# Second level of Strassen's algorithm for two products of the first GEMM, with another order of the visits to its outputs

## The chip, the cores and the metric

The kernel runs on one core of a Trainium2 chip. The metric is the device time of one execution in microseconds (us), the median of several runs. Five engines work side by side, each on its own queue in order: PE (TensorE, matmuls; PEld is its weight loads), DVE (VectorE), ACT (ScalarE), POOL (GpSimd) and SP (SyncE, which here only issues DMAs). They wait for one another through semaphores.

## The reference, cut to what matters

```python
gamma = 1.0 - 2.0 ** (-5.0 - np.arange(H))            # B, H, S, D = 4, 8, 768, 64
for t in range(S):                                      # retention
    state = gamma * state + np.einsum('bhd,bhe->bhde', k[:, :, t], v[:, :, t])
    y[:, :, t] = scale * np.einsum('bhd,bhde->bhe', q[:, :, t], state)
x = y.transpose(0, 2, 1, 3).reshape(B * S, H * D)       # 3072 x 512
h = x @ w_in                                            # 512 x 2048: the first GEMM
g = np.where(h > 0, h, np.exp(np.minimum(h, 0)) - 1)    # ELU
out = g @ w_out                                         # 2048 x 512: the second GEMM
```

All of it is fp32.

## The kernel before, in words

The 3072 tokens are worked through in six blocks of 512 (`tb` 0 to 5; `TB`, `TH` is half of it). For each block the kernel computes the retention (`scores` L256, `states` L275, `outputs` L299), which leaves x transposed in `xb`, then the first GEMM, ELU, and the second GEMM. The order of the instructions on every engine is written out by hand (`manual_schedule`): generators yield at places where other work is put between, and the main loop (L792 to L855) interleaves them. The retention of block tb+1 is cut into five `retention_step`s and lies inside block tb.

Block 0 uses plain matmuls while the weights are decoded. From block 1 on, each GEMM is a Strassen product in Winograd's form. With quarters a of the weights and b of the data, there are seven products M1 = a11 b11, M2 = a12 b21, M3 = s4 b22, M4 = a22 t4, M5 = s1 t1, M6 = s2 t2, M7 = s3 t3, where s and t are sums of quarters. The outputs are C11 = M1+M2, C12 = M1+M6+M5+M3, C21 = M1+M6+M7+M4 and C22 = M1+M6+M7+M5.

- *First GEMM* (`first(n)`, L489; its matmuls are on L501). The 1024 rows of an output quarter are cut into four `n` of 256. For every n, `strassen` (L459) runs the products in the order 1, 2, 6, 7, 5, 3, 4. One product is four matmuls of 128x128 weights with 256 columns and fills one PSUM bank of 128x512. Products 1, 6, 5 and 3 add up in one bank (`pa`, two buffers); 7 and 4 in another (`pd`, one buffer); 2 has `pb`. ACT copies the partial sums out (`kept`, L449 to L451), DVE adds (`plus`, L454 to L456). `elu` (L374) does two activations on ACT (L377, L378) and one operation on DVE (L380), which is held back in the list `later` until the next call. After C12 two subtractions (L513) make T3 and T1, inputs of the second GEMM. `combine_x` (L359) makes t1 to t4 on DVE (L360); `combine_w_in` (L433) makes s1 to s4 once, in block 1.
- *Second GEMM*. In block 1 it is one level (`second`, L554, matmuls on L559); `combine_w_out` (L540) makes the sums for a second level and stores them to `scratch2` in DRAM. From block 2 on it is two levels (`second_twice`, L604, matmuls on L622): each of the seven products is again seven, each of four matmuls with 128 columns into 128x128 of a bank. `inputs` (L607 to L615, operations on L611) makes the inner sums on DVE, `copy` (L628, L630) is a small copy on ACT and `add` (L633, L634) an addition on DVE. The weights of each small product come from DRAM through a ring of 11 tiles `wq` of 256 KB; `fetch_small` (L591) issues the next fetch on SP's queue after each small product. The ring and the pool of the inputs take the memory of the early pools (`stage`, `t4`) once block 1 is over.

The ending of `first(3)` (products 3 and 4) is laid into the start of the second GEMM, and the ending of the last inner product of the second GEMM into the start of the next block.

In block 1 the main loop calls `combine_w_in(n+1)` beside `first(n)`, one operation at each step, and loads the inputs of block 2 (`bring`: `load` on SP's queue and `scale_v`, L238 on POOL). At the end of block 1 it calls `combine_x` and then fills the ring. From block 2 on it issues the loads for the next block at n=0 and n=1, retention steps 0 and 1 at n=2 and 3, and steps 2 to 4 inside the second GEMM behind its inner products 2, 6 and 7.

Of the kernel before, what the change touches and what calls it, by code (L numbers as in the profile page):

```python
# [2 lines left out]

# [5 lines left out]
FP32 = mybir.dt.float32  # L9
# [7 lines left out]
def kernel(  # L17
# [3 lines left out]
    w_bits: bass.AP,  # L21
    scratch: bass.AP,
    scratch2: bass.AP,
    out: bass.AP,
    dims,
):

# [74 lines left out]

    w_a = [const.tile([P, 2, 2, 2, P], FP32, name=f"w_a{n}") for n in range(NQ)]
    w_b = [const.tile([P, 2, 2, 2, P], FP32, name=f"w_b{n}") for n in range(NQ)]
    w_s = [const.tile([P, 3, 2, 2, P], FP32, name=f"w_s{n}") for n in range(NQ)]
    NPIECE = 2 * NQ + NF  # L110
    staged, prepared, decoded = [], [], []

# [108 lines left out]


    xb = const.tile([P, 4, TB], FP32, name="xb")
    xt = [const.tile([P, 2, TH], FP32, name=f"xt{n}") for n in range(4)]
    carry = [const.tile([P, HP, D], FP32, name=f"carry{n}") for n in range(2)]
    held = {}

# [128 lines left out]

    half = [slice(0, TH), slice(TH, TB)]

    def combine_x():  # L359
        sub = lambda o, x, y: nc.vector.tensor_tensor(out=o, in0=x, in1=y, op=ALU.subtract)  # L360
        b11, b12, b21, b22 = (xb[:, 2 * r : 2 * r + 2, half[t]] for r in range(2) for t in range(2))
        sub(xt[0], b12, b11)
        sub(xt[1], b22, xt[0])
        sub(xt[2], b22, b12)
        sub(xt[3], b21, xt[1])


    later = []
# [2 lines left out]
        while later:  # L371
            later.pop(0)()

    def elu(g, h):  # L374

        r = epool.tile([P, 512], FP32, name="r", tag="r")
        nc.scalar.activation(r, h, AF.Relu, scale=-1.0)  # L377
        nc.scalar.activation(r, r, AF.Exp, scale=-1.0)  # L378
        flush()
        later.append(lambda: nc.vector.scalar_tensor_tensor(g, r, -1.0, h, ALU.add, ALU.max))  # L380

    def plain_first():

# [167 lines left out]
                scratch2[j - 1, :, 1024 * k : 1024 * k + 1024], x.rearrange("p k f d -> p (k f d)")  # L551
            )

    def second(tb):  # L554
        def product(j, ps, begin):
            ws = fetched.pop((tb, j))
            for f in range(NF):
                for d in range(2):
                    nc.tensor.matmul(  # L559
                        ps[:, d, :], lhsT=ws[:, 2 * d + f // 4, f % 4, :], rhs=gq[INPUT2[j]][:, f, :],  # L560
                        start=(begin and f == 0 and d == 0), stop=(f == NF - 1), skip_group_check=True,
                    )
            at = ORDER2.index(j) + 3
            if j in (2, 6):
                next_input(j)
            combine_w_out(j, ws)
            if at < 7:
                fetch(tb, ORDER2[at])

        def use(name, h):  # L570
            r, t = int(name[1]) - 1, int(name[2]) - 1
            if name == "C12":
                ot = hpool.tile([P, 2, TH], FP32, name="h", tag="h")
                nc.scalar.copy(ot, h)
                h = ot
            nc.sync.dma_start(out[tb, r, t].rearrange("p d c -> p (d c)"), h.rearrange("p d c -> p (d c)"))

        return strassen(product, use, None)
# [1 line left out]


    RING = 11
    USE = [(1, k) for k in (1, 2, 6, 7, 5)]
    for at in range(1, 7):
        j, before = ORDER2[at], ORDER2[at - 1]
        USE += [(j, 1), (j, 2), (before, 3), (before, 4), (j, 6), (j, 7), (j, 5)]
    USE += [(4, 3), (4, 4)]
    to_fetch = [(tb, j, k) for tb in range(2, NTB) for j, k in USE]
    small_w = []

    def fetch_small():  # L591
        if not to_fetch:
            return
        tb, j, k = to_fetch.pop(0)
        t = ring.tile([P, 4, P], FP32, name="wq", tag="wq")
        if k in (1, 2, 4):
            q = 4 * SLOT[j] + {1: 0, 2: 1, 4: 3}[k]
            nc.sync.dma_start(t.rearrange("p f d -> p (f d)"), scratch[q])
        else:
            n = {5: 0, 6: 1, 7: 2, 3: 3}[k]  # L600
            nc.sync.dma_start(t.rearrange("p f d -> p (f d)"), scratch2[j - 1, :, 512 * n : 512 * n + 512])
        small_w.append(((tb, j, k), t))

    def second_twice(tb, behind_last):  # L604
        quarter = lambda x, r, t: x[:, 4 * r : 4 * r + 4, P * t : P * t + P]
        ts, kept2 = {}, {}

        def inputs(j):
            x, t = gq[INPUT2[j]], tpool.tile([P, 4, 4, P], FP32, name="ts", tag="ts")
            b11, b12, b21, b22 = (quarter(x, a, b) for a in range(2) for b in range(2))  # L610
            sub = lambda o, x, y: nc.vector.tensor_tensor(out=o, in0=x, in1=y, op=ALU.subtract)  # L611
            sub(t[:, 0], b12, b11)
            sub(t[:, 1], b22, t[:, 0])
            sub(t[:, 2], b22, b12)
            sub(t[:, 3], b21, t[:, 1])  # L615
            ts[j] = {1: b11, 2: b21, 3: b22, 4: t[:, 3], 5: t[:, 0], 6: t[:, 1], 7: t[:, 2]}

        def product(j, k, ps, begin):
            name, w = small_w.pop(0)
            assert name == (tb, j, k)  # L620
            for f in range(4):
                nc.tensor.matmul(  # L622
                    ps, lhsT=w[:, f, :], rhs=ts[j][k][:, f, :], start=(begin and f == 0), stop=(f == 3),
                    skip_group_check=True,
                )
            fetch_small()
# [9 lines left out]
        def inner(j):  # L636
# [16 lines left out]
            yield  # L653
            product(j, 3, pa, False)
            nc.scalar.copy(res[:, 0, 1], pa)
            product(j, 4, pd, False)
            add(res[:, 1, 0], pd, u2)
            sum_up(j, res.rearrange("p d t c -> p (d t c)"))
# [23 lines left out]
                add(m, kept2[7], m)  # L682
                store("C21", m)

        inputs(1)
        before = iter(())
        for at, j in enumerate(ORDER2):
            cur = inner(j)
            next(cur)
            if j == 1:  # L690
                yield "tail"
            for _ in before:
                pass
            if j == 2:
                next_input(2)
            if j == 5:
                next_input(6)
            if j == 1:

                next(cur)  # L700
                yield "elu"
                next(cur)
            if at + 1 < 7:
                inputs(ORDER2[at + 1])
            else:
                behind_last()
            if j != 1:
                next(cur)
                next(cur)
            before = cur  # L710
            yield j
        for _ in before:
            pass


    prepare(2)
# [51 lines left out]
            for _ in combine_w_in(0):  # L768
                pass
    combine_x()  # L770
    for j in ORDER2[:3]:
        fetch(1, j)


    def retention_step(tb, step):
# [8 lines left out]
        elif step < 5:  # L784
            outputs_step(tb, step - 2)

    def bring(m):
        load(m)
        scale_v(m)

    tail = iter(())
    for tb in range(1, NTB):  # L792
        more = tb + 1 < NTB
        at_once = more and tb > 1
        for n in range(NQ):
            if at_once and n == 0:
                bring((tb + 1) * CPB)
                bring((tb + 1) * CPB + 1)
            if at_once and n == 1:
                bring((tb + 1) * CPB + 3)  # L800
            cur = first(n)
            for at in range(3):
                next(cur)

            for _ in tail:
                pass
            if at_once and n >= 2:
                retention_step(tb + 1, n - 2)
            side = combine_w_in(n + 1) if tb == 1 and n + 1 < NQ else iter(())
            for s in cur:  # L810
                next(side, None)
                if s == "gap":
                    break
            for _ in side:
                pass
            tail = cur
            if at_once and n == 0:
                bring((tb + 1) * CPB + 2)
            if more and not at_once:
                bring((tb + 1) * CPB + n)  # L820
        if tb == 1:
            cur = second(tb)
            next(cur)
            next(cur)
            for _ in tail:
                pass
            flush()
            for step, s in enumerate(cur):
                retention_step(tb + 1, step)
            combine_x()  # L830
            tail = iter(())
            early.close()
            ring = ctx.enter_context(tc.tile_pool(name="ring", bufs=RING))
            tpool = ctx.enter_context(tc.tile_pool(name="tpool", bufs=2))
            for _ in range(RING):
                fetch_small()
        else:
            cur = second_twice(tb, combine_x if more else lambda: None)
            next(cur)
            for s in tail:  # L840
                if s == "last":
                    break
            next(cur)
            for _ in tail:
                pass
            flush()
            for step, j in enumerate(cur):

                if 0 < step < 4:
                    retention_step(tb + 1, step + 1)  # L850
                if j == ORDER2[-1]:
                    break
            tail = cur
    for _ in tail:
        pass  # L855

# [45 lines left out]
```

## Time and profile before

| | us |
|---|---|
| median of 5 runs | 661.21 (659.58 to 662.9) |
| the profiled execution: its own time | 662.32 |
| its span, from the first to the last instruction | 660.6 |
| PE busy | 639.8 |
| DVE busy | 434.2 |
| ACT busy | 228.9 |
| POOL busy | 23.8 |
| block 2, first to last product (253.23 to 356.08) | 102.85 |
| block 3 (356.08 to 458.27) | 102.19 |
| block 4 (458.27 to 560.46) | 102.19 |
| block 5 to the end of the span (560.46 to 660.6) | 100.14 |

The granted clock of TensorE has a mean of 0.997. A row of the profile gives the line of the kernel, the engine, the operation, the tiles written and read, the shape and a count, then the time. A matmul of the program leaves two records, so counts of matmuls are twice those of the code. What stands in square brackets is how long the engine was idle before, and who ended that.

### The profile page before, as it was taken

How to read it: one execution, taken by the hardware profiler on the slowest of the kernel's cores; microseconds unless marked ns; L12 is line 12 of the kernel's file. 1: busy time of each engine (PE TensorE's matmuls, PEld its weight loads, DVE VectorE, ACT ScalarE, POOL GpSimd, SP SyncE). 2: the span in 40 equal slices, each digit the busy share in tenths (PEclk: the TensorE clock that was granted, in tenths of full speed). 3: DMA queues.
4: the chain of work that ended last, by engine and by line, in shares of the span. 5: the costliest groups of instructions: out<-in, count | busy, mean ns of one | idle time of the engine just before them, and what ended most of it. 6: DMA issues, size and time to landing. Idle time of an engine off the chain costs nothing.

```text
span 660.6 us, 14663 instructions
## 1 busy us (share of the span) xinstructions
PE 639.8 (97%) x6144; PEld 538.1 (81%) x6144; DVE 434.2 (66%) x769; ACT 228.9 (35%) x432; POOL 23.8 (4%) x28
## 2 busy tenths in 40 slices
PE   4899999999999999999899999999999999999997
PEld 4664444558888888889899888999888999888996
DVE  5688778656767635468676457877456868355974
ACT  7467642105441002543112454211544211445211
POOL 1000100000100000200000200000200000000000
PEclk9899999999999999999999999999999999999999
DMA  8648978449214767603789501788700688300793
GB/s 343 233 134 307 324 226 250 133 134 368 100 43 156 263 227 230 279 2 83 239 238 310 234 1 35 211 257 298 304 2 6 197 248 279 120 1 19 223 305 123
DMA packets 63826, 123.65 MB, mean 187 GB/s; under 512 B 5136, under 2 KB 22544, under 8 KB 61712
## 3 DMA queue, kind: packets, MB, share of 16 engines
q1 hardware_dynamic: 63760, 122.70, 55.6%
q8 instruction: 49, 0.80, 0.5%
q14 instruction: 17, 0.14, 0.1%
HBM read 100.66 MB, written 22.02 MB: 186 GB/s over the span
## 4 chain that ended last, share of the span: by engine, by line
PE 93%; DVE 5%; DMA 1%; issue 1%; SPq 0%; ACT 0%; DVEq 0%
PE pa L501 21%; PE pa L622 13%; PE pd L501 10%; PE pd L622 7%; PE hp L400 6%; PE pb L501 5%; PE pa L414 4%; PE pa L559 4%; PE pb L622 3%; PE pd L559 2%; PE kv L286 2%; PE pd L414 2%; PE pb L414 2%; PE y L310 2%; PE y L334 2%; PE sc L264 2%
## 5 line engine op out<-in xcount | busy, mean ns | idle before, releaser
L456 DVE TENSOR_TENSOR h<-pd,m 128x512 f32<-128x512 f32 x42 | 29.1, 692 | 81.9 <-ACT m L451 64.7
L451 ACT COPY m<-pa 128x512 f32<-128x512 f32 x63 | 36.4, 578 | 121.1 <-PE pa L501 85.7
L630 ACT COPY ms<-pa 128x128 f32<-128x128 f32 x84 | 22.3, 266 | 115.4 <-PE pa L622 115.4
L378 ACT ACTIVATE r<-r 128x512 f32<-128x512 f32 x96 | 60.6, 631 | 3.0
L622 PE MATMUL pd<-ts,wq 128*128 128x128 f32 x448 | 60.5, 278 | 0.8 <-DVE res L634 0.8
L622 PE MATMUL pa<-ts,wq 128*128 128x128 f32 x448 | 59.2, 275 | 0.0
L377 ACT ACTIVATE r<-h 128x512 f32<-128x512 f32 x60 | 37.9, 632 | 57.2 <-DVE h L456 57.2
L622 PEld LDWEIGHTS pd<-ts,wq 128*128 128x128 f32 x448 | 54.5, 192 | 2.9 <-DVE res L634 2.6
L622 PEld LDWEIGHTS pa<-ts,wq 128*128 128x128 f32 x448 | 54.8, 192 | 0.2
L622 PE MATMUL pa<-gC,wq 128*128 128x128 f32 x384 | 51.4, 277 | 0.4 <-ACT ms L630 0.4
L380 DVE SCALAR_TENSOR_TENSOR gC<-r,h 128x512 f32<-128x512 f32 x60 | 41.6, 694 | 11.3 <-ACT r L378 11.3
L622 PEld LDWEIGHTS pa<-gC,wq 128*128 128x128 f32 x384 | 47.2, 192 | 1.3 <-ACT ms L630 0.5
L501 PE MATMUL pa<-xt,w_s 128*128 128x256 f32 x160 | 38.4, 383 | 0.0
L238 POOL TENSOR_TENSOR kvn<-kvn,vf 128x512 f32<-128x512 f32 x20 | 21.8, 1089 | 454.2 <-DMA kvn<-in_qkv_dram 360.5
L501 PE MATMUL pa<-xb,w_s 128*128 128x256 f32 x160 | 37.8, 379 | 0.0
L501 PE MATMUL pa<-xb,w_a 128*128 128x256 f32 x160 | 37.8, 379 | 0.0
L501 PE MATMUL pb<-xb,w_a 128*128 128x256 f32 x160 | 37.8, 379 | 0.0
L501 PE MATMUL pd<-xt,w_s 128*128 128x256 f32 x160 | 37.8, 379 | 0.0
L501 PE MATMUL pd<-xt,w_b 128*128 128x256 f32 x160 | 37.8, 379 | 0.0
L501 PE MATMUL pa<-xt,w_b 128*128 128x256 f32 x160 | 37.8, 379 | 0.0
L634 DVE TENSOR_TENSOR res<-pd,ms 128x128 f32<-128x128 f32 x56 | 16.1, 288 | 31.6 <-PE pd L622 29.2
L501 PEld LDWEIGHTS pb<-xb,w_a 128*128 128x128 f32 x160 | 30.4, 190 | 4.1
(121 smaller groups left out, 1096.9 us busy)
## 6 DMA issues: line engine op xcount, KB each, us to landing
wq<-scratch_dram SPq DMA_DIRECT2D x196, 256.0 KB, 4.1
wraw<-in_w_dram SPq DMA_DIRECT2D x16, 1024.0 KB, 5.8
qk<-in_qkv_dram SPq DMA_DIRECT2D x24, 512.0 KB, 8.1
kvn<-in_qkv_dram SPq DMA_DIRECT2D x24, 512.0 KB, 8.4
scratch_dram<-so SPq DMA_DIRECT2D x22, 512.0 KB, 3.2
ws<-scratch_dram SPq DMA_DIRECT2D x7, 1024.0 KB, 7.1
scratch_dram<-w_s SPq DMA_DIRECT2D x8, 512.0 KB, 7.5
out_dram<-res SPq DMA_DIRECT2D x12, 256.0 KB, 4.3
```

The lines of the kernel that those rows point to most:

```text
L238: eng.tensor_tensor(out=kv[:, 1], in0=kv[:, 1], in1=vf[:, i].unsqueeze(2).to_broadcast([C, H, D]), op=ALU.mult)
L377: nc.scalar.activation(r, h, AF.Relu, scale=-1.0)
L378: nc.scalar.activation(r, r, AF.Exp, scale=-1.0)
L380: later.append(lambda: nc.vector.scalar_tensor_tensor(g, r, -1.0, h, ALU.add, ALU.max))
L400: nc.tensor.matmul(hp, lhsT=w[n][:, fi, j // 2, j % 2, :], rhs=xb[:, j, :], start=(j == 0), stop=(j == 3))
L414: nc.tensor.matmul(ops[d], lhsT=wo[:, row, d * P : (d + 1) * P], rhs=g_plain[row * NF + f], start=(f == 0 and row == 0), stop=(f == NF - 1 ...
L451: nc.scalar.copy(m, ps)
L456: nc.vector.tensor_tensor(out=h, in0=ps, in1=m, op=ALU.add)
L501: nc.tensor.matmul(ps[:, fi, :], lhsT=w[:, fi, j2, :], rhs=x[:, j2, :], start=(begin and fi == 0 and j2 == 0), stop=(j2 == 1), skip_group_ ...
L559: nc.tensor.matmul(ps[:, d, :], lhsT=ws[:, 2 * d + f // 4, f % 4, :], rhs=gq[INPUT2[j]][:, f, :], start=(begin and f == 0 and d == 0), sto ...
L622: nc.tensor.matmul(ps, lhsT=w[:, f, :], rhs=ts[j][k][:, f, :], start=(begin and f == 0), stop=(f == 3), skip_group_check=True,)
L630: nc.scalar.copy(m, ps)
```

## The change

It touches blocks 2 to 5 of the first GEMM, and what prepares them in block 1.

1. *M2 and M3 at a second level.* `first_twice(tb, j)` computes M2 (j=2) or M3 (j=3) for all four n at once, 1024x256 by 256x256, as seven products of 512x128 by 128x128: four matmuls with 128 columns each, into 128x512 of a bank. It writes the result straight into the tiles gC11 (M2) and gC12 (M3). Products 1, 2 and 4 read weights that are in SBUF; 5, 6, 7 and 3 read sums which `combine_small` makes on POOL in block 1 (two times four operations of 128x512), stores to a new DRAM tensor `scratch3`, and which come back through the ring: eight more fetches of 256 KB in every block. `combine_x_twice` makes the sums of the data on DVE (four operations of 128x256).
2. *The other five products.* `first_rest` issues products 1, 6, 7, 5 and 4 of an n. `first_end` adds on DVE and puts the sum into the output's tile, from which `elu` then works: C11 = bank + M2, C12 = bank + M3, C21 = bank + copy of M1+M6, C22 = bank + copy of M7 (before: pd + copy of the third sum). ACT copies M1+M6 and M7.
3. *The order.* Product 1 of n+1 stands between products 5 and 4 of n. `elu` may hold back three endings (`depth`), and has three buffers `r`. Product 4 of n=3 stands inside the first inner product of the second GEMM, whose inputs are made just before. The loads for the next block are issued between the parts of the first stage, retention steps 0 and 1 behind n=1 and n=2, and steps 2 to 4 behind inner products 2, 7 and 3.
4. *Block 1.* `combine_w_in(1)` and `(2)` run beside n=0, `(3)` beside n=1, two operations at each step; `combine_small(3)` and `(2)` follow n=2 and n=3; the first three fetches of the second GEMM's weights and the scaling of v come after the loop. The ring is filled inside the last product of the second GEMM (`change`), together with `combine_x_twice`; `combine_x` moves into block 2, in four parts.

```diff
+    W_IN = {2: w_a_[:, :, :, 1], 3: w_s_[:, :, 2]}
+    def combine_small(j):
+        t = stage.tile([P, 4, 4, P], FP32, name="wi", tag="stage")
...
+        tt = lambda o, x, y, op: nc.gpsimd.tensor_tensor(out=o, in0=x, in1=y, op=op)
+        tt(s1, a21, a22, ALU.add)
+        tt(s2, s1, a11, ALU.subtract)
+        tt(s3, a11, a21, ALU.subtract)
+        tt(s4, a12, s2, ALU.subtract)
+        nc.sync.dma_start(scratch3[j - 1], t.rearrange("p k f d -> p (k f d)"))
...
+    def first_twice(tb, j):
+        dst = PLACE[j]
+        place = lambda name, r, t: gq[name][:, 4 * r : 4 * r + 4, P * t : P * t + P]
...
+            for f in range(4):
+                nc.tensor.matmul(
+                    ps[:, f, :], lhsT=lhs[f], rhs=xs[j][k], start=(begin and f == 0), stop=True,
...
+        def plus(r, t, ps, m):
+            nc.vector.tensor_tensor(out=place(dst, r, t), in0=ps, in1=m, op=ALU.add)
+        pa = full(bank("a"))
+        product(1, pa, True)
+        m1 = lift(pa)
+        yield
+        pb = full(bank("b"))
+        product(2, pb, True)
+        plus(0, 0, pb, m1)
+        product(6, pa, False)
+        u2 = lift(pa)
+        pd = full(bank("d"))
+        product(7, pd, True)
+        m7 = lift(pd)
+        yield
+        product(5, pa, False)
+        plus(1, 1, pa, m7)
+        yield
+        product(4, pd, False)
+        plus(1, 0, pd, u2)
+        yield
+        product(3, pa, False)
+        lift(pa, place(dst, 0, 1))
...
+    def first_end(n, name, ps, x=None):
+        g = gq[name][:, 2 * n : 2 * n + 2, :]
+        nc.vector.tensor_tensor(out=g, in0=ps, in1=g if x is None else x, op=ALU.add)
...
+        return lambda: elu(g, g, 3, combine if name == "C22" else None)
...
+    def change():
+        early.close()
...
+        for _ in range(RING):
+            fetch_small()
+        combine_x_twice()
+    cur = second(1, change)
...
+    for tb in range(2, NTB):
...
+        bring(0)
+        rest(0, 1)
+        for _ in tail:
+            pass
+        tail, parts = iter(()), combine_x_parts()
+        for at, j in enumerate(TWICE):
+            cur = first_twice(tb, j)
...
+        for n in range(NQ):
+            rest(n, 6)
+            u2[n] = kept(qa[n])
...
+            if end:
+                end()
+            pop()
+            rest(n, 7)
+            m7 = kept(qd[n])
+            pop(2)
+            if n == 3:
+                next(sec)
+            rest(n, 5)
+            end = first_end(n, "C12", qa[n])
+            other = first_end(n, "C22", qa[n], m7)
+            end()
+            if n < 3:
+                other()
+                rest(n + 1, 1)
+                first_end(n + 1, "C11", qa[n + 1])()
+                rest(n, 4)
+                end = first_end(n, "C21", qd[n], u2[n])
+                pop()
...
+                elif more:
+                    retention_step(tb + 1, n - 1)
+        for _ in range(2):
+            next(sec)
+        other()
+        rest(3, 4)
+        end = first_end(3, "C21", qd[3], u2[3])
+        next(sec)
+        end()
+        flush()
+        for step, s in enumerate(sec):
+            if step in (1, 3, 5):
+                retention_step(tb + 1, 2 + step // 2)
...
```

## The prediction

> **What bounds the kernel now.** I read the page first: its busy table, then the chain that ended last. TensorE is busy 97% of the span and holds 93% of the chain; no other engine exceeds 5% of it.
>
> ```profile
> PE 639.8 (97%) x6144; PEld 538.1 (81%) x6144; DVE 434.2 (66%) x769; ACT 228.9 (35%) x432; POOL 23.8 (4%) x28
> ...
> PE 93%; DVE 5%; DMA 1%; issue 1%; SPq 0%; ACT 0%; DVEq 0%
> ```
>
> Then the timeline of PE in one steady block (tb=3, from 356.08 to 458.27 us). Columns are start, length, line, tiles and count; a program matmul leaves two records, so "x8" is one product of four matmuls. The modelled lengths overlap, so I take the distance between starts.
>
> ```profile
> 364.77 1.89 PE L501 MATMUL pa<-xt,w_b 128*128 128x256 f32 x8
> ...
> 383.77 1.89 PE L501 MATMUL pd<-xt,w_b 128*128 128x256 f32 x8
> ...
> 414.38 1.06 PE L622 MATMUL pa<-ts,wq 128*128 128x128 f32 x8
> ...
> 420.63 1.06 PE L622 MATMUL pa<-ts,wq 128*128 128x128 f32 x8
> ```
>
> Between the first pair lie eleven products of 256 columns: 19.00/11 = 1.727 us each (M below). Between the second lie seven of 128 columns: 6.25/7 = 0.893 us each (P below). A block holds 28 M (48.36) and 49 P (43.76). The gaps that the retention pieces open in that timeline (2.11, 2.11, 1.65, 1.66, 1.18) make 8.71. Sum 100.83 of the block's 102.19: TensorE has at most 1.4 us of waiting in a block to give. Only less matmul time can help much.
>
> The waits of PE name little that could go; the 2.1 us of "issue" (at 326.5) wait for nothing shown.
>
> ```profile
> PE y L334 <- issue: 3.1, 2, 2.1
> ...
> PE pd L622 <- DVE res L634: 0.8, 5, 0.2
> ```
>
> **What the change takes away.** M2 and M3 of the first GEMM are four M each (one per n): 4 x 1.727 = 6.91 us. At the second level each is seven products of four 128-column matmuls, the form of L622: 7 x 0.893 = 6.25. That is 0.66 less, twice in each of four blocks (tb 2 to 5): **-5.25 us**. It lies wholly on the chain.
>
> The rows give 0.893/1.727 = 0.52 for half the columns, so short matmuls cost nothing extra here. [...]
>
> **What it costs beside TensorE.** A hop from PE to ACT or DVE starts 0.2 us after the next product's start, and back to PE it is 0.05:
>
> ```profile
> 652.98 1.06 PE L622 MATMUL pa<-ts,wq 128*128 128x128 f32 x8
> ...
> 654.07 0.27 ACT L630 COPY ms<-pa 128x128 f32<-128x128 f32 x1 [1.52 <-PE pa L622]
> ...
> 654.39 1.16 PE L622 MATMUL pa<-gC,wq 128*128 128x128 f32 x8 [0.35 <-ACT ms L630]
> ```
>
> (652.98 + 0.89 + 0.20 = 654.07; end 654.34; PE at 654.39.)
>
> *Inside the new stage.* A second-level product of the first GEMM fills 128x512, so its copy costs ACT 0.59, not 0.27. Product 6 adds into the bank that product 1 filled, with only product 2 between: 0.20 + 0.59 + 0.05 = 0.84 against 0.89. It fits by 0.05, if ACT has nothing queued. I walked the built program's queue with P1 of M2 at 0: copies at 1.09, 2.88, 3.77, 5.56, 8.24, 9.13, 10.02; DVE's additions (0.69 each) and the four 128x512 subtractions of combine_x land between, with the C11 addition at 10.65 to 11.34 and product 6 of n=0, which needs it, at 11.61. Nothing is late: 0. The writes are strided (128x4x128), which no row shows for ACT; the nearest, DVE's L341 with 128x4x2x64, takes 683 ns against 692 for plain ones, so 0, and at worst one ACT operation for each of four dependent products (see the rivals).
>
> *The plain part.* In each n M6, M7, M5, the next M1 and M4 follow; every operand has one M (1.73) to be read. ACT carries 2 copies and 8 activations, 2 x 0.58 + 8 x 0.63 = 6.2 of 8.6 us; DVE 10 operations, 6.5. It fits: 0. The extra work (per block some 14 DVE operations, 4 of ACT) is hidden here, since DVE has 66.5 busy of 102.2 in block 3 (columns: the stretch and its length, busy PE, PEld, DVE, ACT, POOL with counts, granted clock, DMA share, GB/s):
>
> ```profile
> 356.08:458.27 102.19, 102.02 (x1099) 94.52 (x1098) 66.53 (x123) 33.82 (x73) 4.17 (x4) 1.00 0.53 177
> ```
>
> *Entry to the second GEMM.* This is the new wait. With t=0 at the end of the states' matmuls (L286), DVE has queued seven state additions (0.44 each, from -0.4), three ELU endings (L380) and two subtractions (L513), then two inputs (L611), together 4.6, and only then C12 of n=3: it ends at 7.9, though M5 was done at 5.3. ACT follows strictly in order: two activations (0.66 and 0.63), then the copy of P1 (L630), 9.4. TensorE, after M5, P1, P2 and M4, wants product 6 at 8.7: **0.7 late**. The ending of C21 makes the next product 2 wait 0.2 more. So 0.9 where seven additions stand (tb 2 and 4), 0.5 with six (tb 3, in whose next block one of the 768-step sequences ends and a state is dropped), 0.1 without retention (tb 5): together 2.4, **+2.5** with rounding. What goes there: the old entry's gaps (412.43 to 413.38 and to 414.38 are 0.06 and 0.11 over 0.89), 4 x 0.17 = **-0.7**; and the xb multiplications, moved from behind product 7 to behind 3, free the last product, 453.53 to 454.59 (0.17 over), three times: **-0.5**. The entry's price is bounded by 0 (DVE is ahead) and 5 (twice my lateness).
>
> *Start of tb=2.* Weights for M2 and M3 come through the ring, which may be filled only when the last product of tb=1 has read its stage (253.23). The fetch is issued 0.2 later; landings from DRAM take 2.6 (shortest) to 4.1 us (median), so 256.0 to 257.5, and product 6 wants it at 253.23 + 1.73 + 2 x 0.89 = 256.75. Later ones queue at 0.65 (256 KB at the 403 GB/s seen while these eleven landed) against 0.89 demanded. **+0.4**, between 0 and 0.8. Before, the same fetches had 49 us of cover. In tb 3 to 5 the ring is full in time.
>
> *In tb=1.* The weight combinations (L435) move one n earlier, into DVE's idle 3.7 us before 156.75; the additions of n=1 come 0.35 to 0.5 later and ACT has 0.7 to spare there: 0. GpSimd gains eight 128x512 operations of about 1.04, from some 169 to 178, and two 1 MB stores that go before the fetches of ws on SP's queue; those then issue at about 180, land 7.1 later, and are read at 192: 0. GpSimd disturbs DVE:
>
> ```profile
> 164.37 0.69 DVE L513 TENSOR_TENSOR gT<-gC,gC 128x512 f32<-128x512 f32 x1
> 165.09 1.54 DVE L513 TENSOR_TENSOR gC<-gC,gC 128x512 f32<-128x512 f32 x1
> ```
> ```profile
> 165.04 1.04 POOL L238 TENSOR_TENSOR kvn<-kvn,vf 128x512 f32<-128x512 f32 x1 [1.49 <-DMA kvn<-in_qkv_dram]
> ```
>
> Five such delays of 0.85 make 4.2 us of DVE in a stage (147.3 to 192.2) where DVE is idle 14 of 45 us, and the bank that waits (pd, after C22) has over 3 us. Cost 0, at most 1.5.
>
> **The sum.** -5.25 - 0.7 - 0.5 + 2.5 + 0.4 = **-3.55 us**. The profiled execution took 662.32 (span 660.6, 1.7 around it), so it would be 658.8; the median shown is 661.21, 1.1 below that execution, so I forecast **657.7**.
>
> **Rivals.**
> 1. *DVE is ahead at the entry.* No new waits, the old ones gone: -5.25 - 1.2 = -6.45, 654.8; and if the 2.1 us of "issue" does not recur, 652.7. For it: my lateness rests on one chain of seven dependent additions. Against: the order in DVE's queue is fixed.
> 2. *Given back.* The entry costs twice my figure, the ring 0.8, GpSimd 1.5: -6.45 + 5 + 0.8 + 1.5 = +0.85, 662.1. For it: ACT and DVE serve strictly in order, so one late addition delays what follows. Against: PE's own waits on them in the second GEMM and the retention now total 0.8 + 0.6 + 0.4 = 1.8 us.
> 3. *Slower: the copies of 128x512 fall behind the products of 0.89.* The margin is 0.05. If ACT is one operation (0.6) behind, products 6 and 5 of both M2 and M3 wait 0.6 each: 4 x 0.6 x 4 blocks = 9.6 on top of the sum, 667.3. It decides from 0.9 us of such waits per block (3.5/4) for no gain, and 1.4 for slower. Against: ACT's queue is nearly empty at that place (2 copies of 0.27 just before).
> That the second level isn't carried out is no rival: the built program has 56 matmuls of 128 columns where 32 of 256 stood.
>
> **How the numbers follow.** This measurement can tell about 0.3% from no change, that is 2 us: faster is below 659.2, slower above 663.2. Forecast (655.5 to 659.5) 0.57; rival 1 (652.7 to 655.5) 0.15; rival 2 (659.2 to 663.2) 0.17; rival 3 and above 0.11. Below 659.2: 0.15 + 0.55 = 0.70; within 0.19; above 0.11. The range goes from rival 1's lowest, 652.7, to rival 2's, cut to 661.8.
>
> **What will show it.** Right: pitches of 0.89 through the 14 new products, a block of tb 3 about 1 us shorter, PE waiting on ACT's ms copy for 0.5 to 0.9 once in tb 2 to 4 right after M4 of n=3, and a gap under 1 us near 256.8 on a DMA. Wrong: waits of the new products on their m copies (rival 3); gaps in n=0 to 2; a new "issue" gap; or DVE operations of 1.5 us in n=2 of tb=1 that PE waits for.

## The result, and the profile after

The changed kernel takes a median of 657.74 us (655.14 to 659.5), the kernel before 661.36 (657.82 to 664.18). The ratio is 0.9947, 95% interval [0.9936, 0.9957]: faster by 3.5 us (2.8 to 4.2). The forecast was 657.7. The profiled execution took 659.5, span 657.7.

On the page after, the busy table and the chain that ended last:

```profile
PE 635.2 (97%) x6336; PEld 539.3 (82%) x6336; DVE 468.4 (71%) x825; ACT 237.4 (36%) x448; POOL 36.5 (6%) x36
...
PE 84%; DVE 12%; DMA 2%; issue 2%; SPq 0%; ACT 0%; DVEq 0%
```

PE has 192 records more and 4.6 us less of busy time. DVE, 34 us busier, now has 12% of the chain. Where, the timeline of PE after says; first the new stage and the entry to the second GEMM in block 2:

```profile
255.83 1.06 PE L694 MATMUL pb<-xb,w_a 128*128 128x128 f32 x8
257.25 1.13 PE L694 MATMUL pa<-ts,wq 128*128 128x128 f32 x8 [0.35 <-DMA wq<-scratch_dram]
258.21 1.06 PE L694 MATMUL pd<-ts,wq 128*128 128x128 f32 x8
259.11 1.10 PE L694 MATMUL pa<-ts,wq 128*128 128x128 f32 x8
260.05 1.06 PE L694 MATMUL pa<-xb,w_s 128*128 128x128 f32 x8
...
305.40 1.89 PE L740 MATMUL qd<-xt,w_b 128*128 128x256 f32 x8
308.14 1.16 PE L779 MATMUL pa<-ts,wq 128*128 128x128 f32 x8 [0.85 <-ACT ms L787]
...
311.81 1.41 PE L779 MATMUL pb<-gC,wq 128*128 128x128 f32 x8
313.06 1.06 PE L779 MATMUL pa<-gC,wq 128*128 128x128 f32 x8
```

Starts in the new stage lie 0.89 apart; behind product 5 (259.11) it is 0.94. The gap near 257 is the ring's start: 257.25 - 255.83 - 0.89 = 0.53 late. Product 6 at the entry starts 2.74 after a product of 1.73, so 1.01 late, on ACT's copy, and the product behind such a stop comes another 0.10 late (308.14 to 309.13 is 0.99). The next matrix's product 2 holds PE for 1.25, 0.36 over.

The waits of PE after (us in total, times, longest; these count idle time alone, which is less than the lateness of the start):

```profile
PE pa L779 <- ACT ms L787: 1.7, 3, 0.8
PE pa L779 <- issue: 1.6, 1, 1.6
PE pd L779 <- DVE res L791: 1.1, 5, 0.4
...
PE pa L694 <- DMA wq<-scratch_dram: 0.4, 1, 0.4
```

The "issue" gap is there again, but somewhere else: 334.3 to 335.8, inside a product of L779, where before it was inside the retention's y. Block lengths, from M1 of n=0 to the next block's (block 5: to the span's end), with the "issue" gaps and the ring's gap included. Both are sized by starts: before, the piece of the retention with the gap took 3.99, the same piece in a trace without one 1.56.

| us | block 2 | 3 | 4 | 5 |
|---|---|---|---|---|
| before | 102.85 (2.43 of it "issue") | 102.19 | 102.19 | 100.14 |
| after | 102.60 (1.82 "issue", 0.53 ring) | 100.88 | 101.66 | 99.34 |
| first fetch early (below) | 100.25 (neither) | 100.87 | 101.65 | 99.36 |
| one level, other banks (below) | 101.46 | 102.08 | 103.93 (1.05 "issue") | 100.43 |

From the first row to the third, without "issue": -0.17, -1.32, -0.54, -0.78, in all -2.8. Up to block 2 nothing was gained or lost: it starts at 253.22, before at 253.23. In the other traces it starts between 251.3 and 254.6 (leaving out GpSimd twice, below), and that goes with the granted clock between 12 and 30 us: 251.3 to 251.6 with a mean of 1.00, 252.5 to 253.4 with 0.91, 253.9 to 254.6 with 0.81. The two executions in the first two rows both have 0.91; block lengths leave this spread out.

### The profile page after: what moved, and what is told of

The parts are those of the page before. It is cut to its first block, busy times and chain, and to the rows that moved or that the text cites. A ratio compares the mean times of both kernels' runs of the same rounds, so it can differ in the third digit from the quotient of the medians.

```text
span 657.7 us, 15245 instructions
## 1 busy us (share of the span) xinstructions
PE 635.2 (97%) x6336; PEld 539.3 (82%) x6336; DVE 468.4 (71%) x825; ACT 237.4 (36%) x448; POOL 36.5 (6%) x36
## 4 chain that ended last, share of the span: by engine, by line
PE 84%; DVE 12%; DMA 2%; issue 2%; SPq 0%; ACT 0%; DVEq 0%
PE pa L779 11%; PE pa L740 8%; PE pd L779 7%; PE hp L420 6%; PE pa L434 4%; PE pa L694 4%; PE pa L579 4%; PE pb L740 4%; PE pa L521 4%; DVE ts L656 3%; PE qa L740 3%; PE pb L779 2%; PE pd L694 2%; PE pd L579 2%; DVE gC L394 2%; PE pd L521 2%
## 5 line engine op out<-in xcount | busy, mean ns | idle before, releaser
L779 PE MATMUL pd<-ts,wq 128*128 128x128 f32 x448 | 59.8, 276 | 1.1 <-DVE res L791 1.1
L779 PE MATMUL pa<-ts,wq 128*128 128x128 f32 x448 | 59.4, 275 | 1.3 <-ACT ms L787 1.3
L779 PEld LDWEIGHTS pa<-ts,wq 128*128 128x128 f32 x448 | 54.6, 192 | 2.3 <-ACT ms L787 2.1
L779 PEld LDWEIGHTS pd<-ts,wq 128*128 128x128 f32 x448 | 54.5, 192 | 2.2 <-DVE res L791 2.2
L390 ACT ACTIVATE r<-gC 128x512 f32<-128x512 f32 x64 | 40.0, 625 | 40.0 <-DVE gC L748 40.0
L779 PE MATMUL pa<-gC,wq 128*128 128x128 f32 x384 | 52.0, 278 | 1.9 <-issue 1.6
L779 PEld LDWEIGHTS pa<-gC,wq 128*128 128x128 f32 x384 | 47.3, 192 | 3.3 <-issue 1.7
L394 DVE SCALAR_TENSOR_TENSOR gC<-r,gC 128x512 f32<-128x512 f32 x64 | 45.6, 741 | 0.7 <-ACT r L391 0.7
L242 POOL TENSOR_TENSOR kvn<-kvn,vf 128x512 f32<-128x512 f32 x20 | 22.4, 1127 | 363.8 <-DMA kvn<-in_qkv_dram 276.0
L471 ACT COPY m<-pa 128x512 f32<-128x512 f32 x27 | 15.7, 581 | 67.3 <-PE pa L579 35.5
L656 DVE TENSOR_TENSOR ts<-gC,ts 128x512 f32<-128x512 f32 x48 | 33.0, 688 | 0.8
L656 DVE TENSOR_TENSOR ts<-gC 128x512 f32<-128x512 f32 x48 | 32.9, 685 | 0.0
L434 PE MATMUL pa<-gC,w_s 128*128 128x512 f32 x64 | 30.6, 600 | 0.0
L579 PE MATMUL pa<-gC,ws 128*128 128x256 f32 x128 | 28.6, 381 | 0.0
L579 PEld LDWEIGHTS pa<-gC,ws 128*128 128x128 f32 x128 | 24.1, 190 | 3.4
L779 PE MATMUL pb<-gC,wq 128*128 128x128 f32 x192 | 26.4, 277 | 0.3
L779 PEld LDWEIGHTS pb<-gC,wq 128*128 128x128 f32 x192 | 23.7, 192 | 1.0 <-DVE gC L394 1.0
L748 DVE TENSOR_TENSOR gC<-qa,gC 128x512 f32<-128x512 f32 x8 | 5.5, 692 | 25.0 <-PE qa L740 18.3
```

The source lines that it names most:

```text
L242: eng.tensor_tensor(out=kv[:, 1], in0=kv[:, 1], in1=vf[:, i].unsqueeze(2).to_broadcast([C, H, D]), op=ALU.mult)
L390: nc.scalar.activation(e, h, AF.Relu, scale=-1.0)
L394: nc.vector.scalar_tensor_tensor(g, e, -1.0, h, ALU.add, ALU.max)
L434: nc.tensor.matmul(ops[d], lhsT=wo[:, row, d * P : (d + 1) * P], rhs=g_plain[row * NF + f], start=(f == 0 and row == 0), stop=(f == NF - 1 ...
L579: nc.tensor.matmul(ps[:, d, :], lhsT=ws[:, 2 * d + f // 4, f % 4, :], rhs=gq[INPUT2[j]][:, f, :], start=(begin and f == 0 and d == 0), sto ...
L779: nc.tensor.matmul(ps, lhsT=w[:, f, :], rhs=ts[j][k][:, f, :], start=(begin and f == 0), stop=(f == 3), skip_group_check=True,)
```

## The experiments

My theory: the gain is matmul time, about 5 us; the entry to the second GEMM gives part of it back, since DVE's queue is long there; nothing else costs. The rivals: the new order brings the gain, or the narrow margins of the new stage, the ring and GpSimd cost more than I gave them. Each kernel is an edit of the changed one, and ratios are to the kernel before, so what an edit costs is (its ratio - 0.9947) x 661.36.

**The second level alone undone.** M2 and M3 as eight products of 256 columns.

```diff
-            cur = first_twice(tb, j)
+            cur = first_once(tb, j)
```
```python
ps = bank("ab"[n % 2])
w = w_a[n][:, :, 1] if j == 2 else w_s[n][:, 2]
...
nc.scalar.copy(g[:, 2 * n : 2 * n + 2, :], ps)
```

> The changed kernel with M2 and M3 of the first GEMM as four products of 256 columns each (one level), in the same place, written by ACT into the same sums; order, visits and C22 from a copy of M7 stay. Left out with it: their weights' combinations on GpSimd, their ring fetches, their input combinations on DVE. Theory (the gain is matmul time): eight pitches of 1.73 in place of fourteen of 0.89 in each block, so 657.7 + 5.25 - 0.5 (the ring's start at tb=2) = 662.4 us. Rival (the order and the visits bring the gain): 657.7, at most 658.5.

Measured: 667.05, ratio 1.0087 [1.0053, 1.0121]; neither. The trace names a fault of the experiment, once in each block:

```profile
467.18 1.89 PE L741 MATMUL pb<-xb,w_a 128*128 128x256 f32 x8
469.74 1.99 PE L741 MATMUL pb<-xb,w_s 128*128 128x256 f32 x8 [0.68 <-ACT gC L745]
```

Two products in turn use the bank pb (a piece of M2 is woven into M3). The second waits for ACT's copy and starts 0.83 late (2.56 behind a product of 1.73), the one behind it another 0.10: 4 x 0.93 = 3.7 of the difference. So again, with other banks:

```diff
-            ps = bank("ab"[n % 2])
+            ps = bank(("abdb", "aada")[j - 2][n])
```

> As the one-level run, with the eight products' banks in the order a, b, d, a, b, a, d, a, so that none follows at once on the same bank (there, product n=1 of M3 waited 0.78 us in each block for ACT's copy of product n=3 of M2). Theory (the gain is matmul time, -5.25): 657.7 + 5.25 = 663.0 us, and the 0.78 gaps are gone, -3.1 against 667.05 = 663.9. Rival (what stays of that run's 667 is in the order, which costs more than it brings): 665 or more with gaps elsewhere. Rival 2 (the order brings part of the gain): under 661.

Measured: 663.81, ratio 1.0038 [1.0018, 1.0058], so 6.0 us above the changed kernel, as the theory has it. The table shows it block by block: 101.46 - 100.25 = 1.21, 102.08 - 100.87 = 1.21, 103.93 - 1.05 - 101.65 = 1.23, 100.43 - 99.36 = 1.07, in all 4.7. The order by itself brings nothing: without the second level the kernel is slower than before by 0.2 to 0.6%.

**The lifting copies made twice**, to see the margin of 0.05.

```diff
             nc.scalar.copy(o, ps)
+            nc.scalar.copy(o, ps)
             return o
```

> Each lifting copy of 128x512 of the new stage (P1, P6, P7 and P3 of M2 and M3) is made twice, ACT's second copy onto the first. Theory (margin of 0.05 between copy and product): products 6 and 5 of M2 and M3 wait 0.54 each, 4 x 0.54 x 4 blocks = +8.6, 666.3 us, with these four gaps on ACT in each block. Rival (ACT's copy is done well before its bank is wanted): no gap, 657.7 to 659.

Measured: 666.68, ratio 1.0074 [1.0048, 1.01], 8.4 us above the changed kernel. The size was met, by other waits than I named. The waits of PE:

```profile
PE pa L694 <- ACT m L705: 3.2, 8, 0.4
...
PE qa L741 <- DVE gC L749: 2.6, 4, 0.7
```

Only two waits a block are on the copy, 0.57 each by starts: products 6 and 5 of M2. In M3, products 4 and 3 of M2 are woven in between, and it waits for nothing. The third, 0.82, is M6 of n=0, behind the C11 addition at the stage's end, which has become late. (2 x 0.57 + 0.82) x 4 = 7.8; with what follows each stop the blocks are 2.15 to 2.17 longer than in the table's third row, 8.6 in all.

**C22 from a copy of the sum**, as in the kernel before, but in the new order, where the sum's bank is read for C12 too.

```diff
-            m7 = kept(qd[n])
...
-            other = first_end(n, "C22", qa[n], m7)
+            other = first_end(n, "C22", qd[n], kept(qa[n]))
```

> In the plain part C22 is again the bank of M7 plus a copy of M1+M6+M5, as in the kernel before, so that M4 may write the bank of M7 only behind C22's addition. Theory: no wait in n=0 to 2 (one product stands between), but at the entry (n=3) the addition stands in DVE's queue behind the states, and M4 comes 1 to 1.5 us late in tb 2 and 4, about 0.7 in tb 3; product 6 then waits less. Sum +1.5 to +4: 659.2 to 661.7 us. Rival 1 (the copy of M7 brings nothing): 657.7. Rival 2 (M4 waits in every n): 16 x 0.5, 665 or more.

Measured: 674.53, ratio 1.0208 [1.0176, 1.0241], +17 us. My theory fell; rival 2 holds, and by more than it said: M4 is late in every n, by 0.56 to 0.63 in most, 1.41 once in block 2, and 1.1 to 2.6 at the entries. Rows of DVE, ACT and PE at one M4 of block 4:

```profile
495.39 0.68 DVE L748 TENSOR_TENSOR gC<-pa,gC 128x512 f32<-128x512 f32 x1
496.72 0.69 DVE L748 TENSOR_TENSOR gC<-pd,m 128x512 f32<-128x512 f32 x1 [0.65 <-ACT m L471]
```
```profile
496.10 0.59 ACT L471 COPY m<-pa 128x512 f32<-128x512 f32 x1 [2.45 <-DVE gC L748]
```
```profile
497.47 1.99 PE L740 MATMUL pd<-xt,w_b 128*128 128x256 f32 x8 [0.46 <-DVE gC L748]
```

I had let ACT's copy run beside DVE's C12 addition. It stood idle and started when that addition ended (496.07), and so it did in all 16 n: two readers of one bank came one after the other, then the C22 addition, then M4. The 2.45 of idle time names that addition as what ended it; what set the two readers in turn no run shows. So the copy of M7, from a bank nobody else reads, is what keeps this order free of the wait: none of PE's waits in the changed kernel is on L748.

Some 1.6 of the 17 is not waiting. At the entry of block 2, M4 itself takes 3.42 behind its stop, at a granted clock of 0.53; in block 4, behind a stop little shorter (2.06 of idle time for 2.44), it takes 1.83 at full clock (columns as in the prediction's row of a stretch):

```profile
309.62:313.04 3.42, 3.42 (x8) 2.68 (x9) 1.35 (x3) 1.73 (x4) 0.00 (x0) 0.53 0.03 7
522.23:524.06 1.83, 1.83 (x9) 1.62 (x10) 1.34 (x3) 1.73 (x4) 0.00 (x0) 1.00 0.15 57
```

**The visits of an output close together.**

```diff
-                rest(n + 1, 1)
-                first_end(n + 1, "C11", qa[n + 1])()
                 rest(n, 4)
                 end = first_end(n, "C21", qd[n], u2[n])
+                rest(n + 1, 1)
+                first_end(n + 1, "C11", qa[n + 1])()
```

> In the plain part M1 of the next n stands behind M4, not ahead of it, so that M6 of the next n follows it at once and C11 must be read from the same bank between them. Theory: M6 waits 0.2 + 0.69 + 0.05 = 0.94 us for the C11 addition, three times in each block: 12 x 0.94 = +11, 669 us. Rival (visits need not be apart): 657.7 to 660.

Measured: 665.55, ratio 1.0064 [1.0035, 1.0093], +7.7 us. The wait has the size expected (0.94 by starts), but it comes six times, not twelve:

```profile
PE pa L740 <- DVE gC L748: 4.7, 6, 0.8
```

In blocks 2 to 4 a retention piece stands between M1 and M6 of n=2 and n=3 and covers it; block 5 has no pieces and pays three times. 6 x 0.94 = 5.6, and 0.10 behind each; the entry of block 2 gets 0.7 later as well. By blocks it is 7.1.

**The entry.** First the retention's first two steps one n earlier:

```diff
+        bring(3)
...
-                if n == 0:
-                    bring(3)
-                elif more:
-                    retention_step(tb + 1, n - 1)
+                if more and n < 2:
+                    retention_step(tb + 1, n)
```

> The retention's scores and states of the next block one n earlier (behind n=0 and n=1, not n=1 and n=2), with the load of its fourth chunk before the plain part. Theory (the state additions in DVE's queue make product 6 late at the entry): the waits of 1.0 and 0.63 us on ACT's ms copy in tb 2 and 4 go, 657.7 - 1.6 = 656.1; the waits of 0.3 on C21's ending stay. Rival 1 (ELU endings and subtractions make it late): under half of it goes, 657.0 or more. Rival 2 (moved, not gone): the additions make products of n=2 wait, 657.7 or more.

Measured: 663.04, ratio 1.0036 [1.0014, 1.0058], 5.9 us slower. What the theory says of the entry is right: product 6 waits at none of the four (the one wait on ms that is left, 0.4, is in the last matrix of block 5). But in block 2 something I had not looked at is late:

```profile
279.31 0.79 PE L268 MATMUL sc<-qk 64*64 64x64 f32 x32 [2.15 <-DMA qk<-in_qkv_dram]
281.85 0.86 PE L268 MATMUL sc<-qk 64*64 64x64 f32 x32 [1.74 <-DMA qk<-in_qkv_dram]
```

In block 2 SP issues the ring's eleven fetches first, and the load of the last chunk of q and k goes out at 273.47, 2.5 ahead of the scores; in block 3 it is 7.7 ahead. The scores take 6.64 where 2.02 is usual, and the product behind them 3.29, at a granted clock of 0.54. So in that block scores and states were put behind n=1 together:

```diff
+                if more and n == (1 if tb == 2 else 0):
+                    retention_step(tb + 1, 0)
+                if more and n == 1:
+                    retention_step(tb + 1, 1)
```

> States behind n=1 in every block; scores behind n=0 in tb 3 and 4, but behind n=1 in tb 2, where the scores behind n=0 had waited 3.9 us for their chunks to land. Theory: the scores' wait is gone and the entry's product 6 on time: 657.7 - 1.54 = 656.1 us, the next product 2 still 0.29 late in each block. Rival (the seven additions and four masks together in tb 2 make products of n=2 or the entry wait): 657.5 or more.

Measured: 658.01, ratio 0.9954 [0.9938, 0.9971]; no gain, the rival. The entry is on time; in block 2 the wait is now between the two pieces:

```profile
288.28 0.33 PE L290 MATMUL kv<-kvn 64*64 64x64 f32 x4 [0.54 <-issue]
288.83 2.34 PE L290 MATMUL kv<-kvn 64*64 64x64 f32 x124 [0.22 <-DVE qk L273]
```

Scores and states together take 285.64 to 291.11, 5.47, where two pieces apart take 2.02 each: 1.4 more. The states' banks must first be freed by DVE's masks of the scores (0.22 to DVE's L273; the 0.54 names nobody). In blocks 3 and 4, where the scores stand behind n=0, their data are just in time or late: they take 2.37 and 3.38 for 2.02, with 1.12 on a chunk (idle before 483.00), and these blocks are 0.31 and 0.55 longer than in the table's third row. With M4 of n=3 ahead of product 2, for the other wait of the entry (on C21's ending):

```diff
             m1 = copy(pa)
+            if j == 1:
+                yield
...
-            next(sec)
-        other()
         rest(3, 4)
         end = first_end(3, "C21", qd[3], u2[3])
+        next(sec)
+        other()
```

> At the entry M4 of n=3 stands between products 1 and 2 of the first second-level M1, not behind product 2. Theory (the next matrix's product 2 waits for C21's ending, which is 0.3 late in each block): the ending comes 0.89 earlier, four waits of 0.33 go, 657.7 - 1.3 = 656.4 us; product 6 waits as before. Rival (product 2's wait comes from DVE's queue, not from M4's place): unchanged, 657.7.

Measured: 656.96, ratio 0.9939 [0.9919, 0.9959]; from the changed kernel that cannot be told. The trace can: product 2's wait stays at 0.36, 0.33 and 0.36 in blocks 2 to 4 and goes in block 5 alone (0.29). So the rival holds where states stand in DVE's queue, the theory where they do not.

**The ring's start**: the first weight fetched into an idle tile.

```diff
+        nc.sync.dma_start(xt[3].rearrange("p a b -> p (a b)"), scratch3[name[2] - 1, :, 512 * n : 512 * n + 512])
...
-        for _ in range(RING):
+        for _ in range(RING - 1):
```

> The first fetched weight of tb=2 (product 6 of M2) goes into a tile of the input combinations that is idle since the first GEMM of tb=1, and is fetched 50 us earlier; the ring starts with ten others. Theory: the gap of 0.52 us near 257 goes, the next fetch lands before its product; -0.5, 657.2 us. Rival (the product after it waits in its place): 657.7, gap of 0.3 or more one product later.

Measured: 657.58, ratio 0.995 [0.9931, 0.9968]; no change. Its trace has no gap there, but neither have the traces of the six other kernels that fetch as the changed one does and copy once (states early, states behind n=1, sum copied, visits close, M4 first, GpSimd twice): product 6 starts there 0.89 to 0.90 after product 2. The 0.53 belongs to one execution; in another (M4 first) two products fed by later fetches are 0.2 late together. This run's blocks are the changed kernel's without the two irregular gaps.

**All three**, first with the states one n earlier, then with both pieces behind n=1 in block 2:

> States one n earlier, M4 of n=3 before product 2, and the first fetch of tb=2 early, all three. Theory: the three gains add, -1.6 - 1.3 - 0.5 = -3.4, 654.3 us. Rival (they share their cause, or one of them is given back): 656 or more.

> States behind n=1 (scores as in the run before), M4 of n=3 between products 1 and 2, first fetch of tb=2 early. Theory: with the states out of DVE's queue, C21's ending is bound by M4's place, so now the four waits of 0.3 go too; all entry waits of 2.9 us go, 657.7 - 2.9 = 654.8 us. Rival: 656.5 or more.

Measured: 656.93, ratio 0.9951 [0.9926, 0.9977], and 656.5, 0.9932 [0.991, 0.9954]. In the first, blocks 3 to 5 are 0.32, 1.09 and 0.34 shorter than those of the third row of the table, where the entry's waits make 0.33, 1.09 and 0.29 (with the 0.10 behind block 4's stop): with the states out of the way both kinds go. Block 2 gives its part back, in the first at the chunks, in the second at the masks. The second beats the kernel before; that it beats the changed one (1.0 us by the ratios) is inside the intervals.

**GpSimd's work made twice.**

```diff
+        for _ in range(2):
+            tt(s1, a21, a22, ALU.add)
...
```

> The eight operations of GpSimd that combine the weights of M2 and M3 are made twice (in tb=1). Theory: their own time and DVE's delays beside them stay hidden, but the store behind them stands on SP's queue ahead of the second GEMM's first fetches, which go from 181.3 to some 193 us and land 7.1 later, at 200, where 192.2 is wanted: +8 us, 665.5, in one gap on a DMA near 192. Rival (the fetches are not what is late): 657.7 to 659.

Measured: 668.43, ratio 1.011 [1.0084, 1.0137], +10.8 us, where expected, with a second part:

```profile
191.92 1.89 PE L521 MATMUL pa<-xt,w_b 128*128 128x256 f32 x8
202.54 9.31 PE L579 MATMUL pa<-gC,ws 128*128 128x256 f32 x32 [8.73 <-DMA ws<-scratch_dram]
211.69 1.89 PE L521 MATMUL pa<-xb,w_s 128*128 128x256 f32 x8
```

The store waits for GpSimd on SP's queue and the fetches stand behind it: issued at 195.01 (181.33 in the changed kernel, and 1.5 of that is this execution's later start), first product 8.9 late; the product itself takes 9.15 (6.91), 2.2 more, since its first 4 us pass at a granted clock of 0.50:

```profile
202.54:206.50 3.96, 3.96 (x9) 3.17 (x10) 3.15 (x5) 0.00 (x0) 0.00 (x0) 0.50 1.06 398
```

Fetches 12.2 later cost 8.9, so the changed kernel has 3.3 us to spare here.

## Why the prediction was right, term by term

| term | predicted | measured |
|---|---|---|
| matmuls of M2 and M3 | -5.25 | -4.7 (1.21, 1.21, 1.23, 1.07) |
| old gaps of the entry | -0.7 | -0.7 |
| last product's gap | -0.5 | -0.8 |
| entry to the second GEMM | +2.5 | +3.2 |
| a wait in block 5 | - | +0.2 |
| ring's start | +0.4 | 0 in most executions, 0.5 in one |
| stage, plain part, block 1 | 0 | 0 |
| sum | -3.55 | -2.8 (by blocks -2.8) |

- *The matmul term* is right in kind, 0.5 too large: products 6 and 5 of M2 hold PE for 0.94 instead of 0.89 (twice a block; that is the 0.1 between 1.31 and 1.21). In M3, where one product more stands between, the same products take 0.89, so it is most likely the margin that I called sufficient. Where nothing holds them up, the new rows are 0.893 for 128 columns (260.05 to 262.73 is three), as before.
- *Inside the stage* "nothing is late" held but for these 0.05, and rival 3 was mispriced: four waits on copies, where the doubled copies showed two and one on DVE.
- *The plain part* cost nothing, and here is what I gave least credit: two of the edits that I costed at 0 are what makes it 0. Without one or the other the same second level takes 17 or 8 us more, which is slower than before.
- *The entry* came as the mechanism says, with other sizes. Product 6 is late by 1.0, 0, 0.6 and 0 in blocks 2 to 5 (0.7, 0.3, 0.7 and 0 predicted); product 2 by 0.36, 0.33, 0.36 and 0.29 (0.2, 0.2, 0.2 and 0.1); behind the two stops of product 6 another 0.10 each. C21's ending is late in block 5 as well, without any state in the queue, where M4's place alone sets it.
- *The old gaps* are gone as predicted: the entry's old places show 0.89, and so do the last products of blocks 2 to 4; block 5, where nothing was moved, keeps its 0.17. I had counted 0.17 for a last product and left out the 0.11 behind it (454.59 to 455.59 is 1.00): 3 x 0.28 = 0.8.
- *The wait in block 5* I had not seen: product 4 of the second matrix now waits 0.57 by starts for DVE (0.33 before), since what it waits for stands in DVE's queue behind four additions of L558 and four subtractions of L656 (616.26 to 621.20), and no piece of the retention stands between there.
- *The ring* was sized from the shortest and the median landing. One execution paid 0.5, another 0.2, the rest nothing: a term that should have stood as 0 with a bound of 0.5.
- *GpSimd*: its operations took 1.27 to 1.72 beside DVE, not 1.04, and end at 180.9, not 178; the cover that I named (landing 7.1 after issue, wanted at 192.2) was there.
- *Rival 1* fell at the entry. Its other half, that "issue" may not recur, is a matter of single executions: the one trace of the changed kernel has a gap, six traces of its variants have none.

The blocks of two single executions say -2.8, the medians -3.5 (-2.8 to -4.2); so the forecast's closeness to the median owes part to what the blocks do not show, and the sum that I can account for is 0.7 short of the forecast's -3.55. Among runs of equal mean clock (for the kernel before, those taken beside the experiments) the difference is -2.9 (at 0.997: 660.3 in 26 runs before, 657.4 in 13 after) and -3.6 (at 0.995: 662.1 in 10, 658.5 in 6), so the rest is not resolved. The direction and the mechanism were right; that the number came out to 0.1 is luck, for single terms were off by up to 0.7, to both sides.

## What to carry to other kernels

Another Strassen level pays its arithmetic (4.7 us here) only if every 128-column product finds its operand read in time (the doubled copies cost 8.4): price the place of each copy by the products between writing and rereading a bank, and count reads of one bank by two engines as serial, as they came in all 16 n with C22 from the sum. Work taken out of one queue turns up at the next thing that queue fed: moving the states freed the entry and was paid for at the chunks (3.9 us idle), then at the masks (1.4). Compare block by block, since one irregular gap of 2 us hides most of a gain of 3. And read the granted clock behind a long stop, since the stop can cost more than its length (1.5 to 2.2 us more in three traces).

## What the runs showed of the hardware

*The granted clock behind a stop.* In blocks 1 to 5 three traces have stretches at about half the clock, each behind a stop of TensorE: 0.53 behind 2.44 of idle time (C22 from the sum), 0.54 behind 2.15 and 1.74 in short succession (states early), 0.50 behind 8.73 (GpSimd twice). They cost 1.6, 1.5 and 2.2 us on top of the stop. Stops of 2.12 (before) and 2.06 (C22 from the sum, block 4) had no such stretch; what decides, these runs do not show.

*"issue" gaps.* TensorE stops with nothing in the profile to wait for: 2.12 before, 1.56 after. In three other traces of kernels near the changed one (C22 from the sum, and both with all three edits) it is inside the same product, after five of its eight records, with 1.0; in six (first fetch early, states early, M4 first, copies twice, visits close, GpSimd twice) blocks 2 to 5 have none of 0.4 or more. The two programs with one level have one inside y in block 4 (1.50, 0.74). It keeps to a few places of a program and comes in some executions. No run tells its cause.

*GpSimd and DVE.* Where DVE had two SBUF operands beside a GpSimd operation, one or the other stretched at these places: in block 1 the two subtractions of T3 and T1 behind C22 take 1.69 and 1.64 (before, at the same place, 0.69 each), and GpSimd's scaling of v (L242) behind them 1.49 at 181.89, beside an ELU ending of DVE (181.53), where three others take 1.04.

```profile
175.73 0.68 DVE L394 SCALAR_TENSOR_TENSOR gC<-r,pa 128x512 f32<-128x512 f32 x1
176.44 1.69 DVE L533 TENSOR_TENSOR gT<-gC,gC 128x512 f32<-128x512 f32 x1
178.16 1.64 DVE L533 TENSOR_TENSOR gC<-gC,gC 128x512 f32<-128x512 f32 x1
```
```profile
176.31 1.28 POOL L645 TENSOR_TENSOR wi<-wi,w_a 128x512 f32<-128x512 f32 x1
177.53 1.72 POOL L645 TENSOR_TENSOR wi<-w_a 128x512 f32<-128x512 f32 x1
```

The ending that reads a PSUM operand (175.73) keeps its 0.68, though GpSimd is at work from 174.51 to 176.23.
